# Values of two units written straight into the rows of x, first keys of a third placed earlier, diagonal copies of a fourth on VectorE, moves of x on two queues

## The chip, the cores and the metric

The kernel runs on one core of a Trainium2 chip. The metric is the device time of one execution in microseconds: 598.91 us as the median of three runs (598.01 to 599.17). TensorE (PE) multiplies matrices, VectorE (DVE), ScalarE (ACT) and GpSimd (POOL) work element by element, and SyncE (SP) issues DMAs. Each engine runs its own instructions in order and waits for the others by semaphores. A DMA is issued by an instruction of SP or of ACT; while such an instruction runs or waits, what stands behind it on that engine waits too.

## The reference

An RWKV-6 attention over 4 batches, 8 heads, 768 steps and 48 channels a head, and then an MLP with SiLU over 3072 tokens, 384 in, 2048 wide. All in float32; the two weights arrive as float64.

```python
for t in range(S):                          # B, H, S, D = 4, 8, 768, 48
    kt, vt, rt, wt = (k[:, :, t], v[:, :, t], r[:, :, t], w[:, :, t])
    cur = np.einsum('bhd,bhe->bhde', u[None] * kt, vt)
    y[:, :, t] = np.einsum('bhd,bhde->bhe', rt, state + cur)
    state = wt[:, :, :, None] * state + np.einsum('bhd,bhe->bhde', kt, vt)
x = y.transpose(0, 2, 1, 3).reshape(B * S, H * D)
h = x @ w_in                                # 3072 x 384 by 384 x 2048
out = (h / (1 + np.exp(-h))) @ w_out        # by 2048 x 384
```

## The kernel before

The sequence is cut into blocks of 128 steps (`L`), and a *unit* is one block for two batches: 12 units, numbered 0 to 11. Within a unit the decay is handled by levels of doubling block size, l = 0 to 6: `product` makes the products of w for the next level (`tw`), `grow_keys` and `grow_queries` multiply them into the keys (`tk`, POOL) and queries (`tr`, DVE), `odd_keys` and `odd_ones` copy keys that need no factor (ACT), `start_keys` does the first level on keys (POOL in units 1 and 2), and `scores` multiplies keys by queries on TensorE and keeps the result where a mask says so (DVE, L721, or copies on ACT, L740 and L800). The diagonal comes from `bonus` (r, u and k multiplied), `bonus_sum` (sums over a head), `bonus_spread` (brings the sums to the token's partition; from unit 2 on by four DMAs into `diag` and five small copies into `both_b`, L595 and L597) and `bonus_write` (L604, DVE). Units 0 and 1 start from a state of zero, because they are the first block of their batches.

**From scores to x.** The MLP needs x transposed: 384 channels on partitions as three groups of 128 (`xt`, [128, 3, 256]). A head has 48 channels, so heads don't line up with 128 partitions. In units 0 and 1, `y` multiplies scores by values with each head on 64 partitions of its own (L878, 16 products a unit), ACT copies that to `yt` (L882), and `dense_x` multiplies `yt` by a matrix of zeros and ones, `dense`, that puts every channel in its row of x (L916, 12 products a unit), and the result is copied to `xt` (L918). `dense` is cleared by `clear_dense` and filled by `make_dense`. From unit 2 on `y_state` and `y_values` make `yt` (L869 on ACT) and `move_x` moves it to `xt` by ten DMAs (L928), all issued by SP.

**The MLP.** `up(i, m)` (L1000) multiplies one 256-column piece of w_in by xt of unit i, and ACT writes SiLU of it to `gt` (L1009); its result tile `p_h` has two buffers, so up(i, m + 2) waits for the gt of up(i, m). `down` (L1022; from unit 1's output on `quarter`, L1066) multiplies gt by w_out.

**The weights.** Float64 pieces 0 to 15 (256 columns of w_in, 256 rows of w_out; 768 KB each) land in spare places and are joined to float32: `head_weight` (L223, L225) and `tail_weight` (L231) on ACT, `join_weight` (L242, L243) on DVE, `add_weight` (L255) on POOL. A tail needs the PSUM room that the join before it frees. The piece that takes over a place is loaded after the join that empties it. `down` needs the pieces 8 to 15 in its order.

**The order** is written out by hand in the `do(...)` lists from L1107 on: each engine runs its share of the steps in that order. Units 0 to 2 are interleaved with the weights; from unit 3 on `mix` gives thirteen (later eleven) groups, and a number of `up` and `quarter` steps (`room`) follows each. While TensorE waits for nothing else it is kept busy by `beat` transposes early on. `block_loads(i)` loads w, k and r of unit i in sixteen DMAs each (L123); `clear` wrote zeros to rows of `raw` that those loads don't fill. SP issues nearly all DMAs, in the order of the steps.

**Semaphores of DMAs.** The framework gives each DMA one of eight semaphores in turn, whichever engine issues it, and an issue waits until the DMA that had its semaphore before has landed.

Of the kernel before, what the change touches and what calls it, by code (L numbers as in the profile page):

```python
# [8 lines left out]
F32 = mybir.dt.float32  # L9
# [29 lines left out]
def kernel(  # L39
# [11 lines left out]
    nc = tc.nc  # L51
# [3 lines left out]
    L = 128  # L55
# [241 lines left out]
    parts = sorted({(ch // 128, ch // (2 * D)) for ch in range(DM)})  # L297
    assert len(parts) == KC * 2

    dense = pt.tile([128, H, 2, D], F32, name="ruk", bufs=1).rearrange("p h s d -> p (h s d)").rearrange("p (x t) -> p x t", t=128)  # L300

    def clear_dense():
        nc.gpsimd.memset(dense, 0.0)

# [5 lines left out]

    def make_dense():
        for x, (c, p) in enumerate(parts):
            for e in range(2):
                at, rows = (2 * p + e) * D, slice(PD * e, PD * e + D)
                d0, d1 = max(0, c * 128 - at), min(D, (c + 1) * 128 - at)
                if d0 < d1:
                    nc.scalar.copy(out=dense[rows, x, at + d0 - c * 128:at + d1 - c * 128],
                                   in_=ident[rows, PD * e + d0:PD * e + d1])

# [80 lines left out]
    def clear_all(room):  # L400
        nc.scalar.copy(out=room, in_=zero[:, :, None].to_broadcast(list(room.shape)))
# [3 lines left out]

    def clear(i):

        clear_all(raw[:, i % NSLOT].rearrange("p x b h d -> p (x b h d)").rearrange("p (g d) -> p g d", d=32)[:, :, D - 32:32])
# [463 lines left out]
    def y(i, b):  # L872

        p_yt[i, b] = ps.tile([128, NP, L], F32, name="p_h", bufs=2) if i == 0 else bank("p_m", NP, L)
        for p in range(NP):
            for e in range(2):
                h = 2 * p + e
                nc.tensor.matmul(p_yt[i, b][PD * e:PD * e + PD, p, :], lhsT=whole[i][b][:, h * D:h * D + PD],  # L878
                                 rhs=score[:, i % NSC, e, b * NP + p, :], start=(p == 0), stop=(p == NP - 1))
        if b == 0:  # L880
            yt[i] = pt.tile([128, NP, NB, L], F32, name="yt", bufs=1)
        nc.scalar.copy(out=yt[i][:, :, b, :], in_=p_yt[i, b])  # L882
# [27 lines left out]
    def dense_x(i, b):  # L910

        if b == 0:
            xt[i] = pt.tile([128, KC, TU], F32, name="xt", bufs=1)
        p_x = ps.tile([128, KC, L], F32, name="p_h", bufs=2) if i == 0 else bank("p_m", KC, L)
        for x, (c, p) in enumerate(parts):
            nc.tensor.matmul(p_x[:, c, :], lhsT=dense[:, x, :], rhs=yt[i][:, p, b, :],  # L916
                             start=(x == 0), stop=(x == len(parts) - 1))
        (nc.vector.tensor_copy if (i, b) == (0, 1) else nc.scalar.copy)(out=xt[i][:, :, b * L:(b + 1) * L], in_=p_x)  # L918

    def move_x(i):  # L920

        xt[i] = pt.tile([128, KC, TU], F32, name="xt", bufs=1)
        for h in range(H):
            at = h * D
            while at < (h + 1) * D:
                end = min((h + 1) * D, (at // 128 + 1) * 128)
                row = PD * (h % 2) + at - h * D
                nc.sync.dma_start(out=xt[i][at % 128:at % 128 + end - at, at // 128, :],  # L928
                                  in_=yt[i][row:row + end - at, h // 2].rearrange("p b t -> p (b t)"))
                at = end  # L930
# [162 lines left out]
    def do(*steps):  # L1093
        for fn, *args in steps:
            fn(*args)
# [7 lines left out]
    def back(fn, i, *args):  # L1103
        return both(fn, i, *args)[::-1]
# [3 lines left out]
       (bonus_sum, 0, 0), (clear_dense,), (clear_state,), *back(turn, 0, "w"), (bonus, 0, 2), (bonus_sum, 0, 1), (start_keys, 0, nc.vector, True),  # L1108
       (start_keys, 0, nc.vector, False), (grow_queries, 0, 0), (product, 0, 0, nc.vector), (odd_keys, 0, 1), (grow_keys, 0, 1),
       (make_dense,), (beat, 16))  # L1110

    blocks = block_loads(2)
    others = {1: [(clear, 0), (beat, 6)], 2: [(turn, 1, 0, "r"), (head_weight, 0), (beat, 2)],
              3: [(turn, 1, 1, "r"), (head_weight, 1), (beat, 2)], 4: [(turn, 1, 1, "w"), (reverse_v, 0)],
              5: [(bonus_spread, 0), (bonus_write, 0), (turn, 1, 0, "w")], 6: [*both(turn_in, 1, "k"), *blocks[0:4], (tail_weight, 0)]}
    for l in range(1, NL):
        do((scores, 0, l), *[(grow_keys, 0, l + 1)] * (l + 1 < NL), *others[l])

    do((bonus, 1, 0), (bonus, 1, 1), (bonus, 1, 2), *both(y, 0), (turn_apart, 0), (join_weight, 0), (add_weight,),
       (product, 1, 0), (tail_weight, 1), (turn, 1, 0, "k"), (join_weight, 1), (dense_x, 0, 0), (turn, 1, 1, "k"),  # L1120
       (dense_x, 0, 1), (grow_queries, 1, 0), (odd_ones, 1), (tail_weight, 2), (turn_k, 0), (head_weight, 2),
       (start_keys, 1, nc.gpsimd, True), (add_weight,), (up, 0, 0), (join_weight, 2), *blocks[4:8],
# [6 lines left out]
              3: [(bonus_spread, 1), (reverse_v, 1), (clear, 1), (load_values, 2)]}  # L1129
# [5 lines left out]
    for m in range(1, 4):  # L1135
# [4 lines left out]
    do((scores, 1, NL - 1), (bonus, 2, 0), (bonus, 2, 1), (join_weight, 8), (add_weight,), (bonus_sum, 2, 0), (bonus, 2, 2), (up, 0, 7), *both(y, 1), (turn_apart, 1),  # L1140
       (tail_weight, 9), (turn_k, 1), (dense_x, 1, 0), (head_weight, 9, [0]), (dense_x, 1, 1), (head_weight, 9, [1]),
# [66 lines left out]
```

## Time and profile before

| what | value |
|---|---|
| median of three runs | 598.91 us |
| profiled execution, its own time | 599.11 us |
| span of its instructions | 597.3 us |
| TensorE busy | 587.5 us (98%) |
| VectorE, GpSimd, ScalarE busy | 411.6, 351.5, 232.7 us |
| granted TensorE clock | 1.00 throughout |
| SP's DMA queue | 42.7% of 16 engines' span |

Times in the profile are microseconds from the span's start. A timeline line gives start, length, engine (`SPq` is SP's queue of DMA issues), source line of the kernel, operation, what it writes and reads, the count, and in brackets how long the engine had been idle and what ended that. A line of waits gives who waited for whom, the total, the times and the longest. The chain of waits follows the instruction that ended last back to whatever released it. Each float32 product shows as two matmul records.

### The profile page before, as it was taken

To read this page: it belongs to the slowest core of one execution; us is meant where nothing else is said; L and a number is where in the kernel's file an instruction comes from. 1 tells how busy PE (TensorE), PEld (TensorE's weight loads), DVE (VectorE), ACT (ScalarE), POOL (GpSimd) and SP (SyncE) were. 2 spreads that over 40 slices of the span, in tenths; PEclk is the share of its full clock that TensorE was granted. 3 is DMA by queue.
4 is the path that set the end of the run, shared out by engine and by line. 5 is a ranking of instruction groups with operands and counts; after the bars stand their busy time and mean duration, and the time that the engine had idled before them with its cause. 6 is when DMAs were issued, how large, how long until landed. Compare 5 with 4: busy or idle time off the path is not lost.

```text
span 597.3 us, 14760 instructions
## 1 busy us (share of the span) xinstructions
PE 587.5 (98%) x5790; PEld 527.8 (88%) x5790; DVE 411.6 (69%) x709; ACT 232.7 (39%) x516; POOL 351.5 (59%) x414
## 2 busy tenths in 40 slices
PE   8999999999999999999999999999999999999997
PEld 7787866699899899899899899889889889889997
DVE  7879788798596695596696696686587587542041
ACT  6788874531530540440350351361351251250110
POOL 5998768447578568278378477477477567500000
PEclk9999999999999999999999999999999999999999
DMA  9965794443542543543543643643543531101000
GB/s 227 301 148 149 157 283 75 59 76 51 126 61 66 106 66 52 129 69 53 130 67 55 138 62 52 130 65 52 120 75 52 113 63 27 36 1 28 28 0 27
DMA packets 203078, 53.42 MB, mean 89 GB/s; under 512 B 186752, under 2 KB 194816, under 8 KB 203008
## 3 DMA queue, kind: packets, MB, share of 16 engines
q1 hardware_dynamic: 201424, 51.88, 42.7%
q8 instruction: 46, 0.75, 0.6%
q10 hardware_dynamic: 1584, 0.59, 0.5%
q14 instruction: 24, 0.20, 0.1%
HBM read 43.21 MB, written 5.24 MB: 81 GB/s over the span
## 4 chain that ended last, share of the span: by engine, by line
PE 82%; DVE 5%; POOL 4%; ACT 2%; SPq 2%; DMA 2%; issue 2%; POOLq 0%; DVEq 0%; ACTq 0%
PE p_h L1000 35%; PE p_o L1066 34%; PE p_m L1022 3%; PE p_m L864 2%; PE p_sc L703 2%; PE p_m L843 2%; SPq L123 2%; PE p_m L703 1%; DVE score L721 1%; POOL w_out_sb L255 1%; PE p_sc L892 1%; PE p_sc L819 1%; DMA own<-in_moe_w_out_dram 1%; DMA raw<-in_r_dram 1%; DVE score L604 1%
## 5 line engine op out<-in xcount | busy, mean ns | idle before, releaser
L1000 PE MATMUL p_h<-xt,w_in_sb 128*128 128x256 f32 x1152 | 259.8, 383 | 1.6 <-POOL tk L669 0.7
L1000 PEld LDWEIGHTS p_h<-xt,w_in_sb 128*128 128x128 f32 x1152 | 215.5, 190 | 33.3 <-ACT gt L1009 1.3
L1009 ACT ACTIVATE gt<-p_h 128x512 f32<-128x512 f32 x90 | 53.5, 595 | 172.5 <-PE p_h L1000 172.2
L645 POOL TENSOR_TENSOR tk<-tk,tw 128x256 f32<-128x256 f32 x128 | 93.9, 755 | 35.4 <-issue 21.0
L507 POOL TENSOR_TENSOR ruk<-tokens_rk 128x768 f32<-128x768 f32 (+1 forms) x32 | 51.4, 1616 | 64.4 <-DMA tokens_rk<-in_k_dram 34.6
L1066 PE MATMUL p_o<-own,temps 128*128 128x192 f32 x528 | 87.9, 326 | 0.0
L1066 PE MATMUL p_o<-w_out_sb,gt 128*128 128x192 f32 x508 | 86.4, 326 | 0.0
L1066 PEld LDWEIGHTS p_o<-own,temps 128*128 128x128 f32 x528 | 86.1, 190 | 0.1
L1066 PEld LDWEIGHTS p_o<-w_out_sb,gt 128*128 128x128 f32 x508 | 83.4, 190 | 0.6
L1048 DVE TENSOR_TENSOR temps<-gt 128x256 f32<-128x256 f32 x84 | 50.3, 599 | 25.7 <-ACT gt L1009 25.3
L627 DVE TENSOR_TENSOR tr<-tr,tw 128x512 f32<-128x512 f32 x61 | 54.1, 887 | 14.7 <-PE p_m L703 11.2
L422 POOL TENSOR_TENSOR tw<-tw 128x256 f32<-128x256 f32 (+6 forms) x83 | 40.4, 487 | 35.4 <-DVE tw L374 31.5
L615 ACT COPY tk<-tk 128x256 f32<-128x256 f32 x52 | 21.0, 403 | 102.6 <-POOL tk L645 80.1
L721 DVE COPY_PREDICATED score<-mask,p_sc 128x512 f32<-128x512 int8 x42 | 31.1, 796 | 3.2 <-PE p_sc L703 3.0
L1075 DVE TENSOR_TENSOR partial<-p_o,partial 128x192 f32<-128x192 f32 x33 | 11.7, 355 | 27.8 <-PE p_o L1066 27.8
L1066 PE MATMUL p_o<-w_out_sb,temps 128*128 128x192 f32 x176 | 30.4, 326 | 0.0
L1048 DVE TENSOR_TENSOR temps<-temps,gt 128x256 f32<-128x256 f32 x43 | 29.1, 677 | 1.5
L1075 DVE TENSOR_TENSOR temps<-p_o,partial 128x192 f32<-128x192 f32 x22 | 7.9, 358 | 31.5 <-PE p_o L1066 25.3
L541 DVE TENSOR_REDUCE block_sums<-ruk 128x4 f32<-128x192 f32 (+1 forms) x48 | 24.2, 545 | 7.1 <-POOL ruk L507 7.1
L1066 PEld LDWEIGHTS p_o<-w_out_sb,temps 128*128 128x128 f32 x176 | 28.9, 190 | 0.0
L869 ACT COPY yt<-p_m 48x512 f32<-48x512 f32 x40 | 23.2, 581 | 13.9 <-PE p_m L864 13.1
L703 PEld LDWEIGHTS p_sc<-tr,tk 48*64 48x64 f32 x960 | 17.3, 134 | 12.1 <-issue 7.7
(188 smaller groups left out, 814.2 us busy)
## 6 DMA issues: line engine op xcount, KB each, us to landing
w_out_sb<-in_moe_w_in_dram SPq DMA_DIRECT2D x6, 768.0 KB, 7.6
w_out_sb<-in_moe_w_out_dram SPq DMA_DIRECT2D x4, 768.0 KB, 6.4
own<-in_moe_w_out_dram SPq DMA_DIRECT2D x4, 768.0 KB, 6.1
tokens_rk<-in_r_dram SPq DMA_DIRECT2D x8, 384.0 KB, 4.5
tokens_rk<-in_k_dram SPq DMA_DIRECT2D x8, 384.0 KB, 5.4
tokens_w<-in_w_dram SPq DMA_DIRECT2D x8, 384.0 KB, 6.4
xt<-yt SPq DMA_DIRECT2D x60, 48.0 KB, 1.9
raw<-in_w_dram SPq DMA_DIRECT2D x80, 32.0 KB, 2.2
```

What stands on the lines that cost most here:

```text
L422: engine.tensor_tensor(out=up, in0=t[:, :, 0::2], in1=t[:, :, 1::2], op=ALU.mult)
L507: mul = lambda out, one, two: nc.gpsimd.tensor_tensor(out=out, in0=one, in1=two, op=ALU.mult)
L541: add = lambda out, have: nc.vector.tensor_reduce(out=out, in_=have, axis=mybir.AxisListType.X, op=ALU.add)
L627: nc.vector.tensor_tensor(out=odd, in0=odd, in1=tw[i][l][:, :, 0::2][:, :, :, None].to_broadcast([128, Q, L >> (l + 1), c]), op=ALU.mult)
L645: nc.gpsimd.tensor_tensor(out=out, in0=have, in1=odd_products(i, l, b, *blocks), op=ALU.mult)
L703: nc.tensor.matmul(to, lhsT=tk[i][rows, X[l % 2] + p, x * 64:(x + 1) * 64], rhs=have, start=True, stop=True)
L721: nc.vector.copy_predicated(out=dst, mask=masks[l][:, :, None].to_broadcast([128, NB, NP, ni, c]), data=sc[e].rearrange("p (b q) (i c) -> ...
L869: nc.scalar.copy(out=yt[i][PD * e:PD * e + D, x::2, :, :], in_=p_yt[i, e][PD * x:PD * x + D].rearrange("p (q b) t -> p q b t", b=NB))
L1000: nc.tensor.matmul(p_h[:, a, :], lhsT=w_in_sb[:, c, f * 128:(f + 1) * 128], rhs=xt[i][:, c, :], start=(c == 0), stop=(c == KC - 1))
L1009: nc.scalar.activation(out=gt[i, m], in_=p_h, func=AF.Silu)
L1048: nc.vector.tensor_tensor(out=out, in0=one, in1=two, op=op)
L1066: nc.tensor.matmul(p, lhsT=left(f), rhs=right[:, f, :], start=(f == 0), stop=(f == FH - 1))
```

## The change

It has four parts.

- *Units 0 and 1.* `y`, `dense_x`, `make_dense`, `clear_dense` and `clear` go. `x_products` multiplies values by scores into the rows of x directly: for each half of each group of 128 rows, a product of 64 columns with the scores of the last head in it, and then one of 48, 32 or 16 columns over its first rows with those of the head before. That makes 24 products a unit. `x_copy` copies the result to `xt` (unit 0's second batch on DVE, the others on ACT). `clear_rest` clears on POOL, once, what no load ever writes. In unit 0, product(1, 0) goes ahead of bonus(1, 2), turn_apart ahead of the products; the turns of k and grow_queries(1, 0) go ahead of the copies, tail and head of pieces 1 and 2 shift by a step. In unit 1 the copies come ahead of tail_weight(9), and head_weight(9) is no longer split.
- *Unit 2.* odd_ones goes two rounds of weights earlier, start_keys(2, own) one round earlier and ahead of the products of levels 2 to 6.
- *Unit 3.* The five copies into `both_b` are on DVE (unit 2's stay on ACT; later units use another path).
- *Unit 2's move_x.* The five DMAs of even heads are issued by ACT, the other five by SP.

```diff
+    def clear_rest():
+        for i in range(NSLOT):
+            nc.gpsimd.memset(raw[:, i].rearrange("p x b h d -> p x (b h d)")[:, :, H * 2 * D + PD - D:], 0.0)
...
-        nc.scalar.copy(out=both_b[:, 0], in_=diag[i][0])
+        copy = nc.vector.tensor_copy if i > NTOK else nc.scalar.copy
+        copy(out=both_b[:, 0], in_=diag[i][0])
         for g in range(4):
-            nc.scalar.copy(out=both_b[(3 - g) * 32:(4 - g) * 32, 1], in_=diag[i][1][g * 32:(g + 1) * 32])
+            copy(out=both_b[(3 - g) * 32:(4 - g) * 32, 1], in_=diag[i][1][g * 32:(g + 1) * 32])
...
-    def y(i, b):
...
+    def x_products(i, b):
+        if b == 0:
+            xt[i] = pt.tile([128, KC, TU], F32, name="xt", bufs=1)
+        to = p_x[i, b] = ps.tile([128, KC, L], F32, name="p_h", bufs=2) if i == 0 else bank("p_m", KC, L)
+        have = whole[i][b]
+        places = []
+        for c in range(KC):
+            for row in range(0, 128, PD):
+                at = c * 128 + row
+                last = (at + PD - 1) // D
+                assert at // D == last - 1
+                places += [(c, row, last, PD), (c, row, last - 1, last * D - at)]
+        places.sort(key=lambda place: -place[3])
+        for c, row, h, columns in places:
+            at = c * 128 + row
+            nc.tensor.matmul(to[row:row + columns, c, :], lhsT=have[:, at:at + columns],
+                             rhs=score[:, i % NSC, h % 2, b * NP + h // 2, :], start=True, stop=True)
+
+    def x_copy(i, b):
+        (nc.vector.tensor_copy if (i, b) == (0, 1) else nc.scalar.copy)(out=xt[i][:, :, b * L:(b + 1) * L], in_=p_x[i, b])
...
-    def dense_x(i, b):
...
-                nc.sync.dma_start(out=xt[i][at % 128:at % 128 + end - at, at // 128, :],
+                (nc.scalar if i == NTOK and h % 2 == 0 else nc.sync).dma_start(out=xt[i][at % 128:at % 128 + end - at, at // 128, :],
...
-       (bonus_sum, 0, 0), (clear_dense,), (clear_state,), *back(turn, 0, "w"), (bonus, 0, 2), (bonus_sum, 0, 1), (start_keys, 0, nc.vector, True),
+       (bonus_sum, 0, 0), (clear_state,), (clear_rest,), *back(turn, 0, "w"), (bonus, 0, 2), (bonus_sum, 0, 1), (start_keys, 0, nc.vector, True),
...
-       (make_dense,), (beat, 16))
+       (beat, 16))
...
-    others = {1: [(clear, 0), (beat, 6)], 2: [(turn, 1, 0, "r"), (head_weight, 0), (beat, 2)],
+    others = {1: [(beat, 6)], 2: [(turn, 1, 0, "r"), (head_weight, 0), (beat, 2)],
...
-    do((bonus, 1, 0), (bonus, 1, 1), (bonus, 1, 2), *both(y, 0), (turn_apart, 0), (join_weight, 0), (add_weight,),
-       (product, 1, 0), (tail_weight, 1), (turn, 1, 0, "k"), (join_weight, 1), (dense_x, 0, 0), (turn, 1, 1, "k"),
-       (dense_x, 0, 1), (grow_queries, 1, 0), (odd_ones, 1), (tail_weight, 2), (turn_k, 0), (head_weight, 2),
-       (start_keys, 1, nc.gpsimd, True), (add_weight,), (up, 0, 0), (join_weight, 2), *blocks[4:8],
+    do((bonus, 1, 0), (bonus, 1, 1), (product, 1, 0), (bonus, 1, 2), (turn_apart, 0), *both(x_products, 0), (join_weight, 0), (add_weight,),
+       *both(turn, 1, "k"), (grow_queries, 1, 0), *both(x_copy, 0), (tail_weight, 1), (odd_ones, 1), (turn_k, 0), (join_weight, 1),
+       (start_keys, 1, nc.gpsimd, True), (add_weight,), (tail_weight, 2), (head_weight, 2), (up, 0, 0), (join_weight, 2), *blocks[4:8],
...
-              3: [(bonus_spread, 1), (reverse_v, 1), (clear, 1), (load_values, 2)]}
+              3: [(bonus_spread, 1), (reverse_v, 1), (load_values, 2)]}
...
-       (tail_weight, 9), (turn_k, 1), (dense_x, 1, 0), (head_weight, 9, [0]), (dense_x, 1, 1), (head_weight, 9, [1]),
+       *both(x_copy, 1), (tail_weight, 9), (turn_k, 1), (head_weight, 9),
...
-    others = {0: [(up, 1, 1), (down, 0, 0, 0), *both(turn, 2, "k"), (product, 2, 0), (product, 2, 1)],
-              1: [(up, 1, 2), *both(turn, 2, "r"), *[(product, 2, l) for l in range(2, NL)], *blocks[0:3]],
-              2: [(down, 0, 0, 1), (odd_ones, 2), (start_keys, 2, nc.gpsimd, True), (grow_queries, 2, 0), *blocks[3:6]],
+    others = {0: [(up, 1, 1), (down, 0, 0, 0), *both(turn, 2, "k"), (odd_ones, 2), (product, 2, 0), (product, 2, 1)],
+              1: [(up, 1, 2), *both(turn, 2, "r"), (start_keys, 2, nc.gpsimd, True), *[(product, 2, l) for l in range(2, NL)], *blocks[0:3]],
+              2: [(down, 0, 0, 1), (grow_queries, 2, 0), *blocks[3:6]],
```

In the changed list of unit 1 (the line before the one shown with `x_copy`) `*both(y, 1)` becomes `*both(x_products, 1)`.

More of the change, by code (lines that the diff above doesn't have):

```diff
@@ L294 @@
     mirror = room[:, 4 * L:5 * L]
[L297 to L303, printed above, removed]
     def make_spread():
@@ L309, in make_spread @@
             nc.scalar.copy(out=spread[L // 2:L, s, 1, L - 1 - s::-2], in_=ident[L // 2:L, L // 2:L])
[L311 to L318, printed above, removed]
     tok_all = const.tile([128, NB], I32, name="tok_all")
@@ L398, in turn_out @@
             nc.scalar.copy(out=to, in_=p_tr)
-    def clear_all(room):
-        nc.scalar.copy(out=room, in_=zero[:, :, None].to_broadcast(list(room.shape)))
+    def clear_rest():
+        for i in range(NSLOT):
+            nc.gpsimd.memset(raw[:, i].rearrange("p x b h d -> p x (b h d)")[:, :, H * 2 * D + PD - D:], 0.0)
     def clear_state():
         nc.gpsimd.memset(state, 0.0)
-    def clear(i):
-        clear_all(raw[:, i % NSLOT].rearrange("p x b h d -> p (x b h d)").rearrange("p (g d) -> p g d", d=32)[:, :, D - 32:32])
     def reverse_v(i):
@@ L870, in y_values @@
                            in_=p_yt[i, e][PD * x:PD * x + D].rearrange("p (q b) t -> p q b t", b=NB))
-    def y(i, b):
[L874 to L879, printed above, removed]
-        if b == 0:
-            yt[i] = pt.tile([128, NP, NB, L], F32, name="yt", bufs=1)
-        nc.scalar.copy(out=yt[i][:, :, b, :], in_=p_yt[i, b])
+    p_x = {}
+    def x_products(i, b):
+        if b == 0:
+            xt[i] = pt.tile([128, KC, TU], F32, name="xt", bufs=1)
[15 more added lines that the diff above has]
+        (nc.vector.tensor_copy if (i, b) == (0, 1) else nc.scalar.copy)(out=xt[i][:, :, b * L:(b + 1) * L], in_=p_x[i, b])
     def update(i, b):
@@ L908, in update @@
                 (nc.scalar.copy if i == 0 else nc.vector.tensor_copy)(out=new, in_=p_kv[i][rows])
-    def dense_x(i, b):
[L912 to L918, printed above, removed]
     def move_x(i):
@@ L1138 @@
        (bonus_write, 1))
-    do((scores, 1, NL - 1), (bonus, 2, 0), (bonus, 2, 1), (join_weight, 8), (add_weight,), (bonus_sum, 2, 0), (bonus, 2, 2), (up, 0, 7), *both(y, 1), (turn_apart, 1),
-       (tail_weight, 9), (turn_k, 1), (dense_x, 1, 0), (head_weight, 9, [0]), (dense_x, 1, 1), (head_weight, 9, [1]),
+    do((scores, 1, NL - 1), (bonus, 2, 0), (bonus, 2, 1), (join_weight, 8), (add_weight,), (bonus_sum, 2, 0), (bonus, 2, 2), (up, 0, 7), *both(x_products, 1), (turn_apart, 1),
+       *both(x_copy, 1), (tail_weight, 9), (turn_k, 1), (head_weight, 9),
        (join_weight, 9), (add_weight,), (tail_weight, 10), (head_weight, 10), *both(update, 1), (bonus_sum, 2, 1), (load_rk, 3), (up, 1, 0), *both(turn, 2, "w"))
     blocks = block_loads(3)
-    others = {0: [(up, 1, 1), (down, 0, 0, 0), *both(turn, 2, "k"), (product, 2, 0), (product, 2, 1)],
-              1: [(up, 1, 2), *both(turn, 2, "r"), *[(product, 2, l) for l in range(2, NL)], *blocks[0:3]],
-              2: [(down, 0, 0, 1), (odd_ones, 2), (start_keys, 2, nc.gpsimd, True), (grow_queries, 2, 0), *blocks[3:6]],
+    others = {0: [(up, 1, 1), (down, 0, 0, 0), *both(turn, 2, "k"), (odd_ones, 2), (product, 2, 0), (product, 2, 1)],
+              1: [(up, 1, 2), *both(turn, 2, "r"), (start_keys, 2, nc.gpsimd, True), *[(product, 2, l) for l in range(2, NL)], *blocks[0:3]],
+              2: [(down, 0, 0, 1), (grow_queries, 2, 0), *blocks[3:6]],
               3: [(up, 1, 3), (start_keys, 2, nc.gpsimd, False), (reverse_v, 2), *blocks[6:9]], 4: [(level, 2, 1), (up, 1, 4), *blocks[9:12]],
```

## The prediction

> **What bounds the kernel now.** I read the page first, then TensorE's waits, then the stretches of time around them.
>
> ```profile
> PE 587.5 (98%) x5790; PEld 527.8 (88%) x5790; DVE 411.6 (69%) x709; ACT 232.7 (39%) x516; POOL 351.5 (59%) x414
> ```
>
> TensorE is busy for 98% of the span, so a saving counts only as TensorE work taken out or TensorE idle time closed. Its waits name the idle time (engine, line, releaser: us in total, times, longest):
>
> ```profile
> PE p_sc L703 <- POOL tk L669: 1.5, 1, 1.5
> ...
> PE p_h L1000 <- POOL tk L669: 0.7, 1, 0.7
> ...
> PE p_h L1000 <- ACT gt L1009: 0.6, 1, 0.6
> ```
>
> From 35 us on there are eight gaps: 0.74 at 35.2, 0.55 at 45.0, 0.29 and 0.21 at 54, 0.16 at 63.5, 1.48 at 88.4, 0.63 at 157.4 and 0.08 at 163.5. Nothing else is idle up to the last matmul at 594.1, so whatever time has been won or lost by 163.6 stays to the end. The 1.48 gap, in the timeline of 88 to 98.6 us:
>
> ```profile
> 88.57 1.30 POOL L669 TENSOR_TENSOR tk<-tk,tw 128x128 f32<-128x128 f32 x2
> ...
> 89.51 0.91 ACT L223 ACTIVATE temps<-own 128x768 bf16<-128x768 bf16 x1 [1.56 <-DMA own<-in_moe_w_out_dram]
> ...
> 89.92 0.70 PE L703 MATMUL p_sc<-tr,tk 48*64 48x64 f32 x32 [1.48 <-POOL tk L669]
> ...
> 94.40 1.83 POOL L255 TENSOR_TENSOR w_out_sb<-temps 128x768 uint32<-128x768 uint32 x1 [1.51 <-ACT temps L223]
> ...
> 96.19 1.89 POOL L645 TENSOR_TENSOR tk<-tk,tw 128x256 f32<-128x256 f32 x2
> ...
> 98.51 0.29 PE L703 MATMUL p_sc<-tr,tk 48*64 48x64 f32 x4
> ```
>
> TensorE waits at 89.92 for POOL's L669 (`start_keys` of unit 2). Look at the rest as well: ACT's L223 starts when piece 14 of the weights lands (89.49); from there tail, join, `add_weight` (94.40) and `grow_keys` (96.19, ends 98.08) follow without slack, and scores of level 2 need those keys. They began at 98.51, 0.43 us later. The second gap, first in the chain of waits, then in the timeline:
>
> ```profile
> 154.87 1.75 DMA diag<-own_sums
> ...
> 157.73 2.50 DVE score L604 x2
> ...
> 160.31 0.26 ACT score L800
> ...
> 162.91 0.61 ACT gt L1009
> ...
> 163.56 2.86 PE p_h L1000 x12
> ```
>
> ```profile
> 157.39 1.06 ACT L1009 ACTIVATE gt<-p_h 128x512 f32<-128x512 f32 x2
> ...
> 158.03 6.01 PE L1000 MATMUL p_h<-xt,w_in_sb 128*128 128x256 f32 x25 [0.63 <-ACT gt L1009]
> ```
>
> ACT stood at the five copies of `both_b`, which wait for the DMA of diag, and its two gt copies behind them came late. Then DVE's L604, ACT's twelve L800 and the next gt follow on the same DMA; up(2,6) starts at 163.56 the moment that gt is out. So this DMA already decides at 163.5. SP's timeline shows how it got there:
>
> ```profile
> 132.83 7.74 SPq L928 DMA_DIRECT2D xt<-yt  x10
> 140.62 2.06 SPq L123 DMA_DIRECT2D raw<-in_k_dram  x4
> 142.72 9.22 SPq L123 DMA_DIRECT2D raw<-in_r_dram  x16
> 152.04 0.40 SPq L1079 DMA_DIRECT2D out_dram<-ob  x1
> 152.54 0.38 SPq L1079 DMA_DIRECT2D out_dram<-temps  x1
> 153.01 2.45 SPq L467 DMA_DIRECT2D diag<-own_sums  x4
> ```
>
> SP issues one DMA after another with no pause from 85 us on; diag goes out at 153.01, though its sums were ready at 152.23. SP's own waits are for landings:
>
> ```profile
> SPq L107 <- DMA w_out_sb<-in_moe_w_out_dram: 2.1, 2, 1.7
> ```
>
> Taken apart, each such wait is for the eighth issue before: the issue at 81.55 follows the landing at 81.53 of the one at 76.06. Eight semaphores are dealt in turn, to both queues: SP's issue at 4.31 follows the landing (4.23) of ACT's first.
>
> **The change, part by part.**
>
> *Units 0 and 1, values straight to x.* Removed per unit: 32 matmul records of L878 (1.90 us at 66.40 to 68.30, 0.059 each) and 24 of L916 (68.92 to 71.80, 2.88). Added: 24 products of at most 64 columns, 48 records at 0.059, 2.85. Saved: 1.93 of TensorE per unit. Also gone: four yt copies on ACT (0.59 each), ten of L317 (2.10 together), two of L401 (1.47 each), POOL's clear of `dense` (0.74). Added: two memsets on POOL, 720 elements a partition, 0.74 each by that same row, under POOL's 3.72 idle before 13.72; without that cover 1.5. ACT's removals at 12.75 and 15.94 lie before waits for POOL (15.63, 17.58) and gain nothing. The block loads now wait for the memsets, done by 11, while SP gets to them at 27.68.
>
> In unit 0 turn_apart (0.62) and 24 products follow the scores (29.69), done at 33.2 for 35.15; up(0,0) could start about 34.1 for 35.90. But tail and join of the weights alternate on ACT and DVE, and join 1 now stands behind DVE's copy of x (0.56): join 1 ends near 35.8 (35.03), tail 2 after it, join 3 near 41.9 (42.3). DVE is 95% busy from 40 to 60, so about 0.4 reaches 63.6. product(1,0) (1.04 on POOL) moves ahead of bonus(1,2), into the 1.34 idle before 31.79. In unit 1 the update waits for turn_k, which ACT makes after two x copies and tail 9, near 71.4: update at 71.5 for 71.80, 0.3 won. None of this issues a DMA.
>
> *Unit 2's first keys.* odd_ones (0.66, ACT) moves into the 1.34 idle before 81.55; without it, head 12 is 0.66 late. start_keys (1.30, POOL) moves past add_weight 12 and five products: add 12 goes from 86.46 to about 86.7, with its sum needed only near 91. The 1.48 gap closes. TensorE then comes to scores of level 2 at 97.0 less the 0.7 from above, 96.3, and waits for POOL until 98.1. Landings set that: from 27 to 86 us no SP issue waits for an engine in the trace, so pieces land as before. Won: 0.4, and 0.3 once f 14 of down has waited for add 15 (ends 102.75; needed 103.11). Everything saved so far is capped at 0.3, and 1.8 us could be lost in units 0 and 1 without effect.
>
> *Unit 3's copies on DVE.* ACT's gt come out at 153.7 and 156.3, and the 0.63 gap goes. DVE sat idle there (2.06 before 157.53). The price of a 32x16 copy on DVE is not in the trace: six memsets of 128x16 take 0.21 (0.035 apart), a shuffle of 128x16 0.17. I take 0.17, the row nearest in operands (it reads and writes SBUF): four make 0.7 against ACT's 0.84, so L604 starts 0.15 earlier after the landing; by the memsets 0.6 earlier. The Trainium skill ("VectorE: DVE Perf Modes", section on two Vector instructions with no wait between them) has a copy whose output starts in another quarter of the partitions wait until the one before has finished; the memsets all start at partition 0, so by that rule they are no measure, and by them the sum would be 0.45 better.
>
> *Moves of x, five on ACT.* SP loses five issues at 0.62, 3.1 us, and 0.35 that it waited at 133.4. ACT gets them behind the yt copies (126.03, less the 0.3): 125.8 to 128.9 at 0.62. Behind them wait L1073 (127.80, then 129.2; the quarter that needs its bank starts at 130.16) and odd_ones (130.75): no cost, 1 us of cover. The Trainium skill ("DMA: Bandwidth & Descriptors", Issuing engines are not separate DMA queues) says that a second issuing engine saves only issue time; by that alone SP gains its 3.1, diag goes out by 152.3, and the sum is 0.3 + 0.63 = 0.9 won.
>
> It doesn't count the semaphores. ACT's moves take turns among SP's issues, and SP must then wait for the landing of a move eight turns back. Which turns? At the start ACT's issue has the turn ahead of SP's in each pair, though the source names SP first: the planner deals them by its own clock. The program of before lists ACT's fourth yt copy between the SP issues that the trace has at 118.06 and 118.53, so the planner believes SP some 7 us behind. With turns one by one (move, load, move, load), the load that gets the second move's semaphore is the one issued at 122.51. That move is issued at 126.4 and lands 1.9 later, 128.3. So SP is held 5.8 us. Five moves in a row would hold it 6.5, two loads per move about 4.8; no hold at all is the lower end, 8 the upper (planner 2 us further apart).
>
> Behind the hold on SP: loads of k, v and r, its five moves, diag. Held 5.8, less 3.1 + 0.35, less the 0.63 that the slow issue at 126.95 costs (it falls into the hold), but nothing back for those at 138.88 and 150.13: I take 1.4 late. Moves land near 143.5, up(2,0) needs them at 145.4. diag lands at 158.0 for 156.62; L604 starts at 158.9 for 157.73, the gt is out 5.8 later, 164.7; up(2,6) starts there, for 163.56.
>
> *Sum:* 1.2 us later from 163.6 on. The profiled execution took 599.11 (span 597.3, 1.8 around it), 0.2 over the median of 598.91: 600.3, or 600.1 against the median. I forecast 600.1. About 0.2%, 1.2 us, is what a measurement of this kernel can tell from no change.
>
> **The rivals.**
>
> *SP isn't held (not slower).* If the turns fall so that moves have landed first (ACT's position within about 2 us of SP's, as in the trace), the gain is 0.9 to 1.0: 597.9. For it: at 126.03 SP really is at the issue of 125.96. Against: the program's order of before. It decides once the hold is under some 4.6 us.
>
> *Landings are no cap.* If `grow_keys` came earlier, TensorE's arrival at 96.3 would count, 1.8 more: 598.3 with the hold, 596.1 without. Against: three waits for landings on ACT (76.98, 81.55, 89.51).
>
> *ACT is held.* Were turns dealt in source order, ACT's first move would wait for the landing of the load issued at 128.56, its last for 134; L1073 would come near 135 and the quarter 5 us late: 604. Against: the order at the start.
>
> *The new products don't pay.* Matmuls of 16 or 32 columns slower than 0.059, or a late join, cost nothing until 1.8 us are gone; 1 us above that gives 601.
>
> **How the numbers follow.** Held 0.70 (600.1; its own range 599.2 to 601.8, from holds of 4.8 to 7.5), not held 0.15, no cap 0.07, ACT held 0.04, products 0.04. Slower by over 0.2%, above 600.1: over half of the first (0.38), ACT held and products: 0.46. Faster, below 597.7: 0.12, from a third of the second and half of the third. Same: 0.42. The range goes from 597.6 to 601.8.
>
> **What the profile will show.** Right: no wait of L703 for L669 near 88, TensorE waiting for L645 before 98.1; two gt near 154 and 156; SP with one gap of 5 to 6 us near 122 that ends with a landing of xt; diag issued after 154; up(2,6) waiting about 1 us or more. Wrong: no such SP gap, or L604 before 157.5; or TensorE at scores of level 2 before 97.5.

## The result: 0.47% slower

The changed kernel took 602.11 us (median of 14 runs, 599.02 to 604.80), the kernel before 598.76 us beside it (597.12 to 600.12): a ratio of 1.0047, 95% interval 1.0029 to 1.0065, or 1.7 to 3.9 us more. Forecast were 1.2 more, 600.1, with a range up to 601.8. The median lies 0.3 above that; 598.91, the time that the forecast was made against, times the ratio is 601.7. The direction was right and the path of the loss too. What the sum lacked is a term for TensorE's clock: in the profiled execution the clock falls for a while and that costs 1.7 us, and 7 of the 14 executions show such a fall. The profiled execution took 601.89 us, its span 600.1.

### The profile page after: what moved, and what is told of

The parts are those of the page before. It is cut to its first block, busy times and chain, and to the rows that moved or that the text cites. A ratio compares the mean times of both kernels' runs of the same rounds, so it can differ in the third digit from the quotient of the medians.

```text
span 600.1 us, 14707 instructions
## 1 busy us (share of the span) xinstructions
PE 586.1 (98%) x5774; PEld 524.5 (87%) x5774; DVE 411.8 (69%) x714; ACT 225.1 (38%) x495; POOL 353.6 (59%) x415
## 4 chain that ended last, share of the span: by engine, by line
PE 82%; DVE 4%; ACT 4%; DMA 3%; POOL 2%; issue 2%; SPq 2%; DVEq 0%; ACTq 0%; POOLq 0%
PE p_h L983 35%; PE p_o L1049 33%; PE p_m L845 2%; PE p_m L1005 2%; PE p_sc L684 2%; PE p_m L824 2%; PE p_m L684 1%; SPq L123 1%; POOL tk L626 1%; DMA w_out_sb<-in_moe_w_out_dram 1%; ACT temps L223 1%; DVE score L702 1%; PE p_sc L885 1%; PE p_sc L800 1%; DMA own<-in_moe_w_out_dram 1%
## 5 line engine op out<-in xcount | busy, mean ns | idle before, releaser
L626 POOL TENSOR_TENSOR tk<-tk,tw 128x256 f32<-128x256 f32 x128 | 94.3, 758 | 37.0 <-issue 22.4
L487 POOL TENSOR_TENSOR ruk<-tokens_rk 128x768 f32<-128x768 f32 (+1 forms) x32 | 52.8, 1662 | 63.2 <-DMA tokens_rk<-in_k_dram 37.4
L608 DVE TENSOR_TENSOR tr<-tr,tw 128x512 f32<-128x512 f32 x61 | 56.4, 924 | 14.8 <-PE p_m L684 11.3
L1031 DVE TENSOR_TENSOR temps<-temps,gt 128x256 f32<-128x256 f32 x43 | 26.9, 624 | 1.5
L635 POOL TENSOR_TENSOR tk<-tk,tw 128x256 f32<-128x256 f32 x32 | 27.7, 886 | 0.0
```

Source lines behind the costliest of these rows:

```text
L487: mul = lambda out, one, two: nc.gpsimd.tensor_tensor(out=out, in0=one, in1=two, op=ALU.mult)
L608: nc.vector.tensor_tensor(out=odd, in0=odd, in1=tw[i][l][:, :, 0::2][:, :, :, None].to_broadcast([128, Q, L >> (l + 1), c]), op=ALU.mult)
L626: nc.gpsimd.tensor_tensor(out=out, in0=have, in1=odd_products(i, l, b, *blocks), op=ALU.mult)
L635: nc.gpsimd.tensor_tensor(out=have, in0=have, in1=odd_products(i, l, b, [2, NP * ni]), op=ALU.mult)
L1031: nc.vector.tensor_tensor(out=out, in0=one, in1=two, op=op)
```

## The profile after

The page's busy times first.

```profile
PE 586.1 (98%) x5774; PEld 524.5 (87%) x5774; DVE 411.8 (69%) x714; ACT 225.1 (38%) x495; POOL 353.6 (59%) x415
```

TensorE is busy for 1.4 us less than in before, and ends later. (The slow stretch shown below is counted in these 586.1.) Its waits (engine, line, releaser: us in total, times, longest) have a new first place:

```profile
PE p_h L983 <- ACT gt L992: 2.8, 1, 2.8
...
PE p_m L885 <- ACT kq L808: 1.1, 1, 1.1
```

The waits of up(2,4) for gt (0.63) and of unit 2's first scores for `start_keys` (1.48) are gone, and one wait for gt of 2.82 has come, at up(2,6). (The 1.1 is unit 1's update, further below.) The wait for gt is in the chain of waits, with times from the span's start:

```profile
156.40 1.76 DMA diag<-own_sums
...
158.18 0.17 DVE both_b L578
...
160.37 1.30 DVE score L585
...
164.34 0.61 ACT gt L992
...
164.99 4.34 PE p_h L983 x12
```

This is the chain of before with every step later. diag lands at 158.16 (before 156.62), the four small copies on VectorE end at 158.89, L585 (L604 before) starts at 159.16 (157.73), gt is out at 164.95, up(2,6) starts at 164.99 (163.56). So much is 1.43 us. The rest of the loss stands in the stretches of time around it (start and end, length, then busy us and instruction counts of PE, PEld, DVE, ACT, POOL, the granted TensorE clock, share and rate of the DMA engines):

```profile
157.78:161.19 3.41, 3.41 (x18) 3.00 (x17) 2.88 (x8) 0.61 (x3) 0.00 (x0) 1.00 0.76 194
161.19:164.60 3.41, 0.98 (x5) 0.53 (x3) 1.04 (x2) 3.17 (x11) 1.60 (x1) 1.00 0.96 199
164.60:168.02 3.41, 3.02 (x7) 2.49 (x8) 3.01 (x4) 0.82 (x2) 2.71 (x3) 0.50 0.26 34
168.02:171.43 3.41, 3.41 (x79) 2.84 (x80) 3.38 (x6) 1.46 (x3) 1.71 (x2) 1.00 0.40 51
```

Behind the gap TensorE runs at half its clock for 3.41 us, from 164.605 to 168.018. That is 1.7 us of work lost. Nothing like it stands in the profile of before, where the clock is 1.00 throughout. Other executions of before do have it: of the 113 that ran beside the experiments below, 14 have a mean clock of 0.997 or less.

The reason for the late diag is in SP's timeline,

```profile
118.10 9.04 SPq L123 DMA_DIRECT2D raw<-in_w_dram  x8
127.19 6.82 SPq L123 DMA_DIRECT2D raw<-in_k_dram  x12
...
137.31 3.60 SPq L911 DMA_DIRECT2D xt<-yt  x5
...
143.07 8.83 SPq L123 DMA_DIRECT2D raw<-in_r_dram  x16
151.99 0.39 SPq L1062 DMA_DIRECT2D out_dram<-ob  x1
...
152.96 4.04 SPq L447 DMA_DIRECT2D diag<-own_sums  x4
```

where eight loads from 118.10 on take 9.04 us. The same eight in before's timeline:

```profile
118.06 4.90 SPq L123 DMA_DIRECT2D raw<-in_w_dram  x8
```

SP's waits in the changed kernel have the difference:

```profile
SPq L123 <- DMA xt<-yt: 5.2, 1, 5.2
```

SP's issue of a load waited 5.2 us, from 120.58 to 125.80, for the landing of a move of x, namely the first that ACT had issued:

```profile
123.75 0.63 ACTq L911 DMA_DIRECT2D xt<-yt  x1
...
125.09 1.89 ACTq L911 DMA_DIRECT2D xt<-yt  x3
```

In the program this move holds the semaphore that the fourth DMA of SP behind it has next. (Each semaphore comes round after eight DMAs, and four of the seven between were ACT's.)

How far SP stood behind before at the same issue, its lag, can be read issue by issue: 4.3 us at 125.8 (in before an issue of 1.44 stood in the place of the hold), 4.5 at 137.3, 0.34 at 140.96 after five moves fewer and a slow issue less, 1.3 at 144.5 after a slow issue of 1.42, -0.05 at 152.96, because before's slow issue at 150.13 has no counterpart. Then the first issue of diag itself takes 2.11 us instead of 0.53, and the lag is 1.53. (The list of waits puts 2.0 of it down to VectorE's L483. It can't be that: in before the same issue was through at 153.53, and L503, the same step, started at 154.26. A fetch of instructions runs at that time; see the last section.)

Units 0 to 2, in the timeline, TensorE in unit 1:

```profile
67.08 1.66 PE L871 MATMUL p_m<-score,vt 128*64 128x128 f32 x24
68.66 1.65 PE L871 MATMUL p_m<-score,vq 128*64 128x128 f32 x24
...
72.06 0.89 PE L885 MATMUL p_m<-vt,kq 128*48 128x48 f32 x15 [1.12 <-ACT kq L808]
```

The 24 products take 3.17 us (67.08 to 70.25) for the 4.78 of y and dense_x. Then the update waits for turn_k and starts at 72.06, for 71.80 in before. At 63.6, the end of unit 1's last wait, TensorE was already 0.68 behind before (64.29 for 63.61). None of it shows in the end, though by a narrow margin; unit 2's keys, in the timeline:

```profile
84.26 1.31 POOL L650 TENSOR_TENSOR tk<-tk,tw 128x128 f32<-128x128 f32 x2
...
89.00 0.70 PE L684 MATMUL p_sc<-tr,tk 48*64 48x64 f32 x32
...
95.78 1.89 POOL L626 TENSOR_TENSOR tk<-tk,tw 128x256 f32<-128x256 f32 x2
...
97.72 0.69 PE L684 MATMUL p_sc<-tr,tk 48*64 48x64 f32 x32
```

`start_keys` (L650) is done by 85.6, TensorE reaches the scores at 89.00 without a wait, and the scores of level 2 start at 97.72, right behind `grow_keys` (L626, 97.67): 0.79 ahead of before. TensorE was there at 97.66 and waited 0.06.

## The experiments

Times are medians of each run's executions (9 in e5, 12 in each other); the ratio is to the kernel before on the same chip, with its 95% interval. "Changed" stands for the kernel after.

| run | what it is | us | ratio |
|---|---|---|---|
| e1 | changed, moves all on SP | 599.65 | 1.0013 [0.9987, 1.0038] |
| e2 | changed, one move on ACT | 602.04 | 1.0047 [1.0023, 1.0071] |
| e3 | changed, TensorE kept busy in the gap | 600.32 | 1.0023 [0.9996, 1.0049] |
| e4 | changed, up(2,4) one group earlier | 599.75 | 1.0000 [0.9974, 1.0025] |
| e5 | before, five moves on ACT | 601.47 | 1.0036 [1.0013, 1.0059] |
| e6 | before, copies on VectorE | 599.51 | 1.0014 [0.9989, 1.0038] |
| e7 | e1 and e4, unit 3's moves earlier | 598.43 | 0.9991 [0.9972, 1.0010] |
| e8 | changed, ten moves on ACT | 601.60 | 1.0040 [1.0024, 1.0056] |
| e9 | before, unit 2's keys earlier | 599.83 | 1.0011 [0.9984, 1.0037] |
| e10 | before, products of units 0 and 1 | 600.15 | 1.0021 [1.0003, 1.0039] |
| e11 | e4, unit 3's moves earlier | 599.31 | 1.0005 [0.9983, 1.0027] |
| e12 | e1 and e4, unit 4's moves earlier | 597.19 | 0.9978 [0.9962, 0.9995] |

One execution differs from the next by a us and more, so a single row of this table tells little below 0.3%; the verdicts rest on what the traces show beside it.

### Moves of x: none, one, five or ten on ACT, and five in the kernel before

```diff
-(nc.scalar if i == NTOK and h % 2 == 0 else nc.sync).dma_start(out=xt[i]...
+nc.sync.dma_start(out=xt[i]...                                        # e1
+(nc.scalar if i == NTOK and h == 0 else nc.sync).dma_start(...        # e2
+(nc.scalar if i == NTOK else nc.sync).dma_start(...                   # e8
```

e5 has the changed line, and nothing else of the change, in the kernel before.

> The changed kernel with all ten moves of unit 2 on SP again. Theory (SP held by ACT's moves, and the late diag then makes a gap of 2.8 us that also drops TensorE's clock): no gap in SP's issues near 120 to 126, diag issued near 153.0 as in before, landing near 156.6, up(2,6) near 163.4 with a gap of about 1.2 instead of 2.8, no stretch at clock 0.5, so 1.5 + 1.7 less than the changed kernel: about 598.6, level with before. Rival (the copies on VectorE or the products are what is late, the moves are hidden): gap and slow clock stay, 601 to 602.

> The changed kernel with only the first of the five moves on ACT. Theory (the hold ends when the first of ACT's moves lands, whatever their number): SP still held 4 to 5.5 us before 126, and only 0.6 of issue time saved instead of 3.1, so diag about 2.5 us later still, up(2,6) near 167, about 604. Rival (each move costs its share of the hold): a hold of about 1 us, diag near 151.7, about 598.

> The changed kernel with all ten moves of unit 2 on ACT. Theory (the hold lasts to the landing of ACT's first move, whatever their number; it was 3.5 us with one move and 5.2 with five): 5 to 6 us again, while SP saves another 3.1 us of issue time, so diag goes out as soon as its sums are there, near 151.7 to 153, the gap before up(2,6) shrinks from 2.8 to about 1 and the clock stays: about 599. Rival (the hold grows with the number of moves): 8 us or more, and 602 or more.

> The kernel before with nothing but the five moves of even heads on ACT. Theory (the hold on SP alone makes the loss): SP held 4 to 5 us up to the landing of ACT's first move near 126 to 127, diag landing about 1.5 later than 156.6; the gap at 157.4 grows from 0.63 to about 2.1, since the copies of diag still stand on ACT, and up(2,6) starts near 165.1; 1.5 more than before, 600.4, and 1.7 more than that in runs where the clock falls. Rival (the loss needs the other parts of the change): 598.9 or less.

SP's waits for landings of moves between 100 and 170 us were none in e1, and in e2, e8 and e5, in this order (each fence is one kernel's answer on SP's waits):

```profile
SPq L123 <- DMA xt<-yt: 3.5, 1, 3.5
```

```profile
SPq L123 <- DMA xt<-yt: 7.9, 5, 5.6
```

```profile
SPq L123 <- DMA xt<-yt: 3.1, 1, 3.1
```

So the hold belongs to the moves on ACT. It comes with that part alone, which makes the kernel before 0.36% slower (601.47, for 600.4 expected and 602.1 with a fall of the clock; TensorE's gap before up(2,4) is 2.21, for 2.1), and goes with it. It doesn't grow in step with the number of moves: 3.5 us with one, 5.2 with five, and with ten 5.6 at the first and four small ones behind it, 7.9 together. In each of these traces and the changed kernel's the first hold ends with the release of the semaphore of ACT's first move (125.80 with five, 126.85 with one, 125.65 with ten, 127.69 in e5).

How late diag gets by it differs from one execution to the next, since SP's slow issues fall in different places. Counted from SP's store just ahead of the hold (117.62 in before), the last move of diag lands 38.5 to 39.2 us later in the five traces with all moves on SP in which that landing is on record (before, e1, e7, e10, e12), and 39.3 to 40.5 us later in the five with five moves on ACT (the changed kernel, e3, e4, e5, e11): 1.0 on average. The changed kernel's profile, with 1.5, stands at the upper end.

With one move the hold was to be 4 to 5.5 and the time 604; it was 3.5, and 602.04. The step that was missing: with one move all seven turns between are SP's, so it is held at its eighth DMA behind that move and not at its fourth, 4 x 0.49 = 2.0 us further on. 5.2 less 2.0 is 3.2, for 3.5 measured.

In e1 diag goes out at 151.63 and lands at 155.94, and TensorE's wait before up(2,6) shrinks:

```profile
PE p_h L983 <- ACT gt L992: 0.6, 1, 0.6
```

It starts at 162.76, 2.2 earlier than in the changed kernel, at full clock, and the span falls from 600.1 to 597.2. 598.6 was expected for 599.65 measured (598.98 in the profiled execution). By its time alone e1 can't be told from before, nor its interval be parted from the changed kernel's; it is the traces that part them.

The ten moves of e8 let SP wait for diag's sums (it stood idle 1.35 us in front of that issue), and TensorE waits just 0.2 for gt, as expected. But the time is not the 599 that was expected. TensorE waits in two other places:

```profile
PE p_o L1049 <- ACT partial L1056: 1.2, 1, 1.2
...
PE p_h L983 <- DMA xt<-yt: 0.8, 1, 0.8
```

The first is ACT's copy of a quarter (L1056, L1073 before) behind its ten issues, at 129.6: the cover of 1 us that the prediction gave the five moves there was used up by ten. The second comes up again below.

### The clock

```diff
+    def fill(n):
+        p = banks["p_sc"][turns_of["p_sc"] % 2][:, 0:L]
+        for x in range(n):
+            nc.tensor.transpose(p, ident, ident)
...
+            steps[13].insert(0, (fill, 18))      # ahead of up(2, 6)
```

> The changed kernel with 18 transposes (0.108 us each, 1.9 us) on TensorE ahead of up(2,6), which leave 0.9 us of the gap idle. Theory (the gap itself costs 1.4 more than in before and the slow clock behind it another 1.7): up(2,6) still near 165.0, clock 1.00 throughout, 1.7 less than the changed kernel: about 600.2. Rival (the clock has nothing to do with the gap's length or costs nothing): no change, 602.

The stretches of time of e3, of the same length as those shown of the changed kernel and at the same distance from the first grant of the clock:

```profile
161.57:164.99 3.42, 2.67 (x21) 2.33 (x21) 0.67 (x2) 3.31 (x10) 1.81 (x1) 1.00 0.79 141
164.99:168.40 3.41, 3.41 (x38) 2.77 (x41) 3.38 (x4) 0.93 (x3) 3.28 (x3) 1.00 0.27 36
```

600.32 us were measured for 600.2 expected. up(2,6) starts at 164.71, 0.28 earlier than in the changed kernel; the gt is nearly as late as there, the clock stays at 1.00, and the last matmul ends at 595.11 for 596.87. So of the 2.8 us of the loss between these profiles some 1.5 to 1.7 is the clock. Over all executions it is less, because the clock does not fall in each: those of the changed kernel without a fall have a median span of 598.3, for 596.8 in before, which is the 1.5 of the chain alone. Falls are in 7 of 14 executions for 14 of 113, at 1.7 each an estimated 0.6 on average. Time outside the span adds 0.3 (last section). That makes 2.4 of the 2.9 us between the mean times of the changed kernel and of those 113; the rest is open. e3 agrees: 598.2 is its median span without a fall, and falls are down to 3 of 12.

The same fall of the clock is in the profiles of e2 (2.91 us of gap) and of e5:

```profile
157.35:160.76 3.41, 1.36 (x66) 1.02 (x64) 0.32 (x3) 1.40 (x6) 0.00 (x0) 1.00 0.30 47
160.76:164.18 3.41, 3.26 (x8) 2.65 (x9) 2.91 (x3) 2.55 (x10) 0.00 (x0) 0.50 1.02 268
```

### The order on ACT

```diff
-        room = (1, 1, 0, 2, 1, 1, 1, 1, 1, 2, 2, 1, 1) if i < NPAIR ...
+        room = (1, 1, 0, 2, 1, 1, 1, 1, 1, 3, 1, 1, 1) if i < NPAIR ...
```

> The changed kernel with up(2,4) placed one group earlier, ahead of the scores of levels 5 and 6 of unit 3, so that its gt on ACT no longer stands behind the copies that wait for diag. Theory (the late diag costs only through that order): no gap at 162, up(2,6) near 162.2, clock 1.00, 2.8 + 1.7 less than the changed kernel: about 597.5, and SP still held 5 us. Rival (another wait for the late diag takes its place, at up(2,7) or at the later products of unit 3): 599 or more.

No gap is left at 162; up(2,6) starts when up(2,5) is done, though diag lands at 157.55 only and SP was held 4.5 us. The span falls by 3.3, to 596.8, where 4.5 was expected, and most of the rest went into a wait for VectorE at 179 (0.96 us) that hadn't been there:

```profile
PE p_o L1049 <- DVE temps L1058: 1.0, 1, 1.0
```

VectorE works with hardly a pause from diag's landing on to the copy that TensorE waits for there, and ends it 22.34 us behind the landing: at 179.89 here, at 179.88 in e7 (landing 157.54), at 178.89 in e12 (landing 156.55, no wait). So this wait is one for the late diag too, and the rival holds in part. The median, 599.75 for 597.5 expected, is level with before; on average e4 has 0.5 us more time outside the span than before (2.29 for 1.80). The late diag cost what it cost because two gt stood behind the twelve copies on ACT that wait for it.

### The other parts alone

e9 has only the earlier first keys of unit 2, e10 only the products of units 0 and 1, e6 only the copies on VectorE; all three are otherwise the kernel before (the edits are those of the diff).

> The kernel before with only unit 2's first keys placed earlier. Theory (the landing of weight piece 14 sets when the keys of level 2 are grown, so the gap only moves): the gap of 1.5 at 88.4 goes, TensorE waits instead for the grown keys until about 98.1 for 98.5, and the whole gains 0.4: 598.5. Rival (no cap by landings): scores of level 2 start at 97.1 and the whole gains 1.5: 597.4.

> The kernel before with only the values of units 0 and 1 straight into the rows of x; the other three parts as in before. Theory (what units 0 and 1 lose or win by 64 is taken up by the wait at 88): TensorE 0.7 late at 63.6 as in the changed kernel, the gap at 88 shorter than 1.5 by as much, scores of level 2 within 0.5 of 98.5, the whole within 0.5 of before. Rival (the loss reaches the end): 0.7 or more above before, 599.6; or (the saved 3.9 us of products count) 597 or less.

> The kernel before with only unit 3's five copies of diag on VectorE. Theory: the gap of 0.63 at 157.4 goes, but the same DMA decides one step later: L604 starts at most 0.15 earlier, the gt 5.8 us behind it, so up(2,6) starts near 163.4 and TensorE waits about 0.5 in front of it; the whole gains 0.1: 599.0, no measurable change. Rival (the gap is won): 0.6 less and no gap before up(2,6): 598.4.

TensorE's waits in e9, then in e10, then in e6:

```profile
PE p_h L1000 <- DMA xt<-yt: 1.6, 1, 1.6
...
PE p_h L1000 <- ACT gt L1009: 1.1, 1, 1.1
```

```profile
PE p_h L983 <- DMA xt<-yt: 0.7, 1, 0.7
...
PE p_sc L684 <- POOL tk L650: 0.4, 1, 0.4
```

```profile
PE p_h L1000 <- ACT gt L1009: 1.1, 1, 1.1
```

*Keys (e9).* The gap at 88 is gone, and TensorE doesn't wait at 98 either (keys grown at 96.94, scores at 97.49): the cap by landings that the theory put there isn't seen in this execution, and it is by 0.8 to 1.8 us in others (e2, e7, e11), since the landing of piece 14 differs by as much (from 88.3 in e9 to 90.2 in e2). What was won is taken later: up(2,4) waits 1.10 for the gt behind diag, and up(4,0) waits 1.56 at 238.9 for unit 4's moves of x, which SP issues at 231.5 to 237.8 in its unbroken row of DMAs (the last of them also lands 1.1 later than in before, at 240.30). No gain is left, as far as 12 runs can tell; neither 598.5 nor the rival's 597.4 came out.

*Products (e10).* Behind before at 63.97 by 0.36 us (0.7 was expected), and the wait at 88 is 0.41 for 1.48: taken up, as expected. The gain then goes at 239, 0.74. Its span is that of before (medians 597.5 and 597.35); its time is 0.21% above, with an interval that ends at 0.03%. The means differ by 0.87 us: 0.29 of it lies outside the span (last section), and 3 of its 12 executions have a fall of the clock, for 3 of 32.

*Copies (e6).* The gap at 157 goes and comes back one step later: TensorE waits 1.09 before up(2,6), more than the 0.5 expected, because it arrived 1 us earlier in this execution (its wait at 88 was 0.43 with code that is before's). That wait is thus worth 0.4 to 1.5 us from one execution to the next, and one profile showed its upper end.

### A better version

Unit 4's moves were the next limit. In before the last of them lands at 239.20. TensorE starts up(4,0) at 238.29 and needs that one about 1.1 us into it (in e7 it starts at 237.59 and stops at 238.72), so there is almost nothing to spare; whoever gains ahead of it waits there.

```diff
-  *bonus_steps(i, 4, 5), (move_x, i - 1)],
+  *bonus_steps(i, 4, 5), *at(i > NPAIR, (move_x, i - 1))],       # e7, e11
+  *bonus_steps(i, 4, 5), *at(i != NPAIR + 1, (move_x, i - 1))],  # e12
...
+        if i == NPAIR - 1:                                       # e7, e11
+        if i == NPAIR:                                           # e12
+            groups[-1].insert(-5, (move_x, i))
```

All three have e4's `room`; e7 and e12 also have e1's line, and e11 has the change's.

> The changed kernel with up(2,4) ahead of the scores of levels 5 and 6 as in the fourth run, and unit 3's ten moves of x on SP placed ahead of the 24 loads that stood before them (those moves landed at 238.7 in the fourth run, up(3,0) was ready for them at 238.7). Theory (SP's order is the second limit, and moving this one thing lifts it): moves landed by 228, no gap near 239, the hold near 120 to 125 as before but without effect; about 598.3. Rival (the 24 loads that go behind the moves are late in their turn): a new gap of TensorE after 239, 599.5 or more.

> The same, and all ten moves of unit 2 on SP. Theory (the hold is covered in the other run already, so that taking it away gains nothing more, unless DVE's wait near 179 hangs on it): no gap at 162, none near 239, 597.8 to 598.3, some 0.7 below before. Rival (each of the two limits is replaced by a next one of the same size): 599 or more.

> The changed kernel with unit 2's ten moves of x on SP, up(2,4) ahead of the scores of levels 5 and 6, and unit 4's moves (they are the ones that landed at 239.7 in the last run, where TensorE waited 1.12 for them at up(4,0); the two runs before had moved unit 3's by mistake) ahead of the last 12 loads that stood before them. Theory (unit 4's moves cap what TensorE wins before 238): they land near 233, no gap near 239, about 1 less than the last run: 597.0 to 597.6, 1.2 below before. Rival (the loads put behind are late in their turn, or a next wait of the same size): a gap after 240 and 598.4 or more.

e11 and e7 moved the wrong transfers. Those that land near 239 are unit 4's, and the edit took unit 3's, 12 loads earlier (176.4 for 181.2). So TensorE still waits at 239, 0.63 in e11 and in e7:

```profile
PE p_h L985 <- DMA xt<-yt: 1.1, 1, 1.1
```

Their 599.31 and 598.43 are level with before. e12 moved the right ones. SP's timeline in e12 shows them eight us earlier, and from 98 us on no wait of TensorE's above 0.05 us is left:

```profile
223.30 6.72 SPq L911 DMA_DIRECT2D xt<-yt  x10
```

It took 597.19 us, 0.22% less than before (0.05 to 0.38) and with that 0.7% less than the changed kernel (0.9978 over 1.0047): all parts of the change but the moves on ACT, and two edits of the order. Whether these two edits would gain as much on the kernel before, without any part of the change, was not run; nor do the intervals of e7 and e12 part the two.

## Why the prediction was right, and where it was wrong

- *SP held by ACT's moves (0.70).* Right. Forecast: 5.8 us, from 122.5 to 128.3, for the landing of the second move. Measured: 5.2, from 120.6 to 125.8, for that of the first. So the mechanism was right, and which DMA held the semaphore was not. ACT issues the first move between two yt copies (123.75), 2 us before the place that the working gave it, since the move needs only two of the four copies, and the eighth turn behind it fell to SP's fourth DMA.
- *Diag 1.4 late.* 1.53, though by other terms, so the agreement is partly luck. The terms that the working lists (5.8 less 3.1, 0.35 and 0.63) make 1.7 and not the 1.4 that it took. What came instead: the hold was 0.6 shorter, two slow issues had shifted, and one of them, 1.5 long, fell on diag itself. The working gave nothing back for the later slow issues; they moved, and 1.37 came back and 1.58 went. The sign "diag issued after 154" didn't come either: its first issue began at 152.96, and it is that issue's length which made diag late.
- *The chain behind it.* diag 158.0, L604 158.9, gt and up(2,6) 164.7 were forecast; 158.16, 159.16, 164.95 and 164.99 came.
- *Copies on VectorE.* 0.17 each, four in 0.7 were forecast; 0.166 and 0.70 came. The row nearest in operands was the right one, and the memsets the wrong. The gap of 0.63 went, and added itself to the one behind.
- *The sum.* 1.2 more was forecast, 1.43 is what up(2,6) was late. The step that failed is the sentence "1.2 us later from 163.6 on": it takes a gap to cost its own length. The working had closed the gaps at 88 and 157, and all that had been won had to stand in front of up(2,6) as one gap of 2.82, 2.43 of it within one stretch of 3.41. The clock then fell, 1.7 us, and no term or rival had it. In the 7 executions in which it didn't, the span is 1.5 above before's, near the forecast.
- *Units 0 and 1.* 0.4 ahead at 63.6 was forecast, 0.68 behind came. The products took 0.066 to 0.068 a record and not 0.059 (3.2 us for 2.85), turn_apart 1.06 for 0.62, and scores of unit 0 began 0.85 later at 16.5, in this execution, after a late landing. join 1 ended at 36.9, not 35.8. The rival "products don't pay" was right in its parts, and the cushion of 1.8 us made it free, as the prediction put it. But it was a close thing: TensorE came to level 2 at 97.66 and not at 96.3, the keys were there 0.42 sooner, and 0.06 of the cushion was left. The sizes were wrong; that the conclusion held is luck in part. Nor is the 0.68 a price of the products alone: that point lies between 63.58 and 64.66 in the four traces without them and between 63.71 and 64.35 in the ten with them.
- *Unit 2's keys.* The gap closed and TensorE waited for the grown keys: right, though for 0.06 us only. At 98 it was 0.79 ahead, not 0.4: piece 14 landed 0.42 sooner (89.07 for 89.49), against "pieces land as before", and 0.43 that TensorE had arrived late in before was gone. e9 adds that this cap is not there in every execution.
- *SP isn't held: 597.9.* e1 is this rival: 599.65, level with before, so 1.7 too good. It left out that diag still makes TensorE wait 0.56 before up(2,6). In e1's trace a wait of 0.36 for VectorE at 272 comes on top; in other runs unit 4's moves limit what reaches 238.
- *ACT is held (0.04).* Not so: its five moves went out within 2.6 us, and L1056 (L1073 before) behind them ran at 127.20.
- *The chances.* A third of 0.15 and half of 0.07 make 0.09, not the 0.12 given for "faster".
- *The page on DMA.* By the rule that a second issuing engine saves only issue time (the Trainium skill, "DMA: Bandwidth & Descriptors", Issuing engines are not separate DMA queues) the sum was 0.9 won. The runs show a second engine that saves 3.1 us of issue time and costs 5.2 of holding.

Between 165 and the end TensorE won back 0.4 of the 3.1 us that up(2,6) and the clock make together; where is open.

## What to carry to other kernels

A second queue is not free where both draw their semaphores from one row: the busy queue is held until the slow engine's DMA has landed, 3.5 us by a single one here and 5.2 by five, so count the turns between the two and compare the times at which each queue gets there. Where several small waits of TensorE are closed ahead of one that stays, they come together in front of it, and a gap that takes 2 us and more out of one clock window of 3.4 can cost its length and half such a window besides. Before an early gain is counted, follow the busiest in-order queue to the end: here its transfers for a later unit had no slack, and no gain could be told from the noise until they were moved too.

## What the runs showed of the hardware

*The clock falls after a window of 3.413 us that is mostly idle.* Every fall ahead of the last matmul in these traces lasted 3.413 us, and began a whole number of such windows after the clock was first granted (160.426 us = 47 windows in the changed kernel and in e2, 153.6 = 45 in e5). In the windows ahead of them TensorE was busy 0.98, 0.50 and 1.36 us of 3.41. Windows with 1.85 (e9, at 238.4), 1.93 (before, at 87.2) and 2.13 us (e11, at 96.0, where a gap of 1.82 is cut by the edge) were followed by full clock. The windows in which the kernels end say the same: 1.39 us busy (e11, from 594.3 on) was followed by a fall, 1.73 (e7, from 592.9 on) was not. So the limit lies between 1.39 and 1.73 us of 3.41, and the place of the gap in the window decides. That may be why 7 of the 14 runs of the changed kernel show a mean clock of 0.996 or 0.997 (one window at half clock in 600 us is 0.997) with a median span of 600.9, and 7 one of 0.999 or more with 598.3. The Trainium skill ("TensorE: Matmul & The Clock Gate", Part 1) has the same window of 3413 ns, free-running, and lets the clock fall after at least one idle window; here a window that was 40% busy was enough.

*Instruction fetches slow down issues.* SP's issues of 1.0 to 2.1 us, for 0.45 to 0.6 else, nearly all coincide with transfers of 16 KB on the instruction queue (153.10 in the changed kernel, with the issue of diag at 152.96). Which issue is hit depends on what stands ahead on SP: with the products of units 0 and 1 alone it is one of diag's (e10, 1.48 us at 152.91), with the five moves on ACT alone a load before it (e5, 151.90). It isn't the same issue in each execution either: e4 has the changed kernel's DMAs, and there it is the store ahead of diag (152.06). The Trainium skill ("Runtime: NRT & Kernel Launch", Instruction fetch mechanics) calls the cost of crossing such a block mostly hidden; on this queue, which issues without a pause, it is 0.6 to 1.6 us in the changed kernel's trace.

*Time outside the span.* It was 1.8 us (1.7 to 1.9) in all runs of before, e5, e6 and e9, and of e3. In the other kernels with the new products of units 0 and 1, 3 to 8 of 12 runs had 2.0 to 3.5. The mean was 2.14 in the changed kernel, so 0.3 of its loss. Why e3 has none of it, and what runs there, stays open.
